# Chunk-selected attention and a hard-swish MLP in one kernel: longer K rows, a different split of the batch 0 bounds, a third transposed group by DMA, another last tile, and a new order

## The chip, the cores and the metric

The kernel runs on one core of a Trainium2 chip. The time is the device time of one execution in microseconds. One execution was also taken by the hardware profiler; its times are us from the start of the profiled span. The engines are PE (TensorE: matmuls and transposes; PEld is its weight load), DVE (VectorE), ACT (ScalarE), POOL (GpSimd) and SP (SyncE, which here issues nearly all DMAs; a few early ones come from ACT).

## The reference

Four batches, 8 heads, 768 positions, head size 64. K is cut into 24 chunks of 32 positions. For each query an upper bound of its scores with each chunk is worked out from the chunk's minimum and maximum, the 6 best chunks at or before its own are kept, and attention runs on those alone, causally. The result, as 3,072 rows of 512, goes through a two-layer MLP.

```python
k_min, k_max = np.min(k_chunks, axis=3), np.max(k_chunks, axis=3)
ub = np.sum(np.maximum(q * k_min, q * k_max), axis=-1)      # per query and chunk
ub = np.where(causal, ub, -1e9)
top_chunks = np.argsort(ub, axis=-1)[..., -6:]
scores = np.where(sel & causal_positions, scale * q @ k.T, -1e9)
x = softmax(scores) @ v            # as 3072 x 512
h = x @ w_in                       # 512 x 2048
g = h * np.clip(h + 3, 0, 6) / 6
out = g @ w_out                    # 2048 x 512
```

Queries 0 to 191 have at most six chunks, so bounds are needed for the 576 others.

## The kernel before, in words

**An order written out.** All work is a list of tokens (`ORDER`), each of which calls one small function; the functions' instructions are appended to their engines' queues in the list's order, and each engine runs its own queue in that order, waiting where an operand is not there or a buffer is not free. A token's last letter is a PSUM place: a, b, c are tiles of two banks, x and y single banks. There is no planner at build time: the list is the schedule, for the queues of SP and POOL too.

**Batch 0 (four head pairs, tokens in capitals).** `AQ`, `LK`, `LQ`, `LV` load half of a head's q, k or v (96 KB, rows of 256 bytes, L379 and L388). `KT`, `QT` transpose them on PE (L398) with an identity that POOL makes (`PI`); `MX`, `MN` reduce K's chunks to maximum and minimum on DVE (L412); `KB`, `QB` cast to bf16 on ACT. `UH.i.h` computes the bounds of pair i (L440): the low half (h=0) has 192 queries, two column groups of 96; the high half (h=1) has 384, two column groups of 192. `UB` adds the causal bias (L446; bias made by POOL, `PB`, L266 to L271), `TH` transposes (L454), `T8` takes the top eight (L461), `SE` compares (L465), `LH` and `MT` bring the mask back (L471, L475). The chunk indicator `EM`, which turns a mask into additions to the scores, is cut by POOL (`PC`, L278, L280) and copied to four partition groups (`EG`, L288).

**Batches 1 to 3 (six quads of four heads, n = 2 to 7, tokens in small letters).** `lk.n`, `lq.n` load K or Q of a quad, four DMAs of 192 KB, 32 positions to a partition group per head, rows of 256 bytes (L222), into one of three slabs of the staging buffer, which batch 0's halves also use. `kd`, `qd` turn 32 x 32 blocks on DVE (L228); `kb`, `qb` cast on ACT (L303); `mx`, `mn` reduce (L311), `kx` takes the span (L316), `rp` the positive part of Q (L322). `ud.n` computes the bounds (L333, 128 small matmuls), `us`, `tr`, `tm`, `se`, `tb` bias, turn, select and turn back on DVE, `mv` moves mask rows on POOL (L363), and `SQ.n.u` computes the scores of four heads for one of six units (L510, L514).

**Attention and MLP.** `ex` is the exponential (ACT, L520), `af` the causal cut on POOL (L527), `A`, `B` the products with V for the low and high three query blocks (L543), `na`, `nb` the normalisation (DVE, L560, L563) into x. A group g of 384 rows (two to a batch) is transposed either on PE (`X.g.n`, two steps of six transposes, L576, copied by DVE, `xe`, L580: groups 0 to 2) or by three DMA transposes on SP (`xt.g`, L569: groups 3 to 7). `wl`, `wc` load a 1 MB weight chunk (L238) and cast it on POOL (L242): chunks 0 to 3 are w_in, of which `H.g.f` needs chunk f // 2; 4 to 7 are w_out, of which `O.g.t.n` needs chunk 4 + n. `H.g.f` is a hidden step (L587, 8 matmuls), `hu` (ACT, L595) and `gt` (DVE, L598) the gate, `O.g.t.n` a quarter of an output tile's projection (L625, 4 matmuls; n needs the gates 2n and 2n + 1), `ot` its unload on ACT (L632), `st` its store on SP (L636). One tile, `LAST`, is computed as two halves of 256 columns, each unloaded and stored by itself (L613 to L616). `LAST` is the tile of the list's last `st` token, which is (7, 0); but its steps stand ahead of those of tile (7, 2).

Of the kernel before, what the change touches and what calls it, by code (L numbers as in the profile page):

```python
# [9 lines left out]
A = mybir.AluOpType  # L10
# [5 lines left out]
P = 128  # L16
CH = 32
# [17 lines left out]
PW AQ.2.0.1 LK.0.0.0 PT PI PO LK.0.1.1 AQ.0.0.1 PR Z.y.6 PZ PF PB LK.0.0.1 KT.0.0.b PC AQ.0.0.0 MX.0.0 EG.2 LK.1.0.1  # L35
MN.0.0 EG.0 LK.1.0.0 PA EG.1 QT.0.0.y AQ.1.0.1 EG.3 AQ.1.0.0 LK.0.1.0 AQ.2.0.0 RP.0.0 RN.0.0 KT.1.0.a MN.1.0 MX.1.0
KB.0.0 QB.0.0 QT.1.0.x KT.0.1.y RP.1.0 KB.1.0 RN.1.0 UH.0.0.c UH.1.0.b QB.1.0 MN.0.1 KB.0.1 LQ.0.1.1 UB.1.0 UB.0.0
MX.0.1 LQ.0.1.0 QT.0.1.a RA.0.1 QB.0.1 RP.0.1 TH.1.0.b T8.1.0 TH.0.0.c LQ.3.0.1 T8.0.0 QT.2.0.x RP.2.0 SE.1.0
LQ.3.0.0 QT.3.0.y RP.3.0 LK.3.0.0 RN.2.0 SE.0.0 LK.2.0.1 UH.0.1.a LK.2.0.0 KT.2.0.b RN.3.0 LK.3.0.1 UB.0.1 QB.2.0
MN.2.0 QB.3.0 KT.3.0.c LQ.2.1.0 KB.3.0 LH.1.0.a MX.2.0 MT.1.0 KB.2.0 LQ.2.1.1 QT.2.1.y UH.2.0.a RP.2.1 RA.2.1 QB.2.1  # L40
MX.3.0 LK.3.1.0 LH.0.0.b MN.3.0 TH.0.1.x LQ.1.1.1 MT.0.0 S.0.1.b ex.0.1 UB.2.0 T8.0.1 SE.0.1 S.0.0.a ex.0.0 LK.1.1.0
af.0.0 LQ.1.1.0 QT.1.1.c RN.1.1 QB.1.1 TH.2.0.y RP.1.1 LH.0.1.b LK.1.1.1 KT.1.1.x T8.2.0 SE.2.0 UH.3.0.a LH.2.0.y
MT.0.1 LV.3.0.1 KB.1.1 LV.0.0.0 LK.2.1.1 S.1.1.b UB.3.0 ex.1.1 af.1.1 MT.2.0 MN.1.1 S.0.5.c LK.2.1.0 MX.1.1 KT.2.1.y
MN.2.1 MX.2.1 S.1.0.a TH.3.0.x ex.0.5 ex.1.0 UH.1.1.b T8.3.0 S.2.1.c SE.3.0 UB.1.1 UH.2.1.a UB.2.1 af.0.5 LH.3.0.b
MT.3.0 TH.1.1.x af.0.1 ex.2.1 KB.2.1 af.2.1 T8.1.1 S.2.0.c TH.2.1.y af.1.0 ex.2.0 lk.2 LV.3.0.0 S.0.3.b ex.0.3
S.0.4.c SE.1.1 T8.2.1 SE.2.1 LH.1.1.x MT.1.1 LK.3.1.1 ex.0.4 LV.0.0.1 VC.0.0 KT.3.1.a MN.3.1 A.0.y LV.1.0.1 na.0
KB.3.1 S.3.1.b ex.3.1 S.3.0.c LQ.3.1.0 LV.1.0.0 LQ.3.1.1 QT.3.1.x MX.3.1 RN.3.1 ex.3.0 VC.1.0 af.2.0 A.1.y na.1
RP.3.1 LH.2.1.b MT.2.1 S.1.3.a ex.1.3 S.1.4.c LV.2.0.0 kd.2.1 X.0.0.y xe.0.0 ex.1.4 UH.3.1.b UB.3.1 af.3.1 mx.2.1
S.1.5.a S.1.2.c QB.3.1 VC.3.0 af.3.0 A.3.y na.3 LV.2.0.1 ex.1.5 af.1.3 ex.1.2 VC.2.0 A.2.x S.0.2.b ex.0.2 TH.3.1.y
na.2 S.2.3.c ex.2.3 T8.3.1 LV.0.1.1 SE.3.1 wl.0 S.2.5.a X.0.1.x xe.0.1 S.2.2.b ex.2.2 LH.3.1.y MT.3.1 wc.0 af.0.2  # L50
wl.1 kd.2.0 mx.2.0 H.0.1.c hu.0.1 ex.2.5 gt.0.1 mn.2.0 af.1.2 af.0.3 LV.0.1.0 VC.0.1 B.0.0.x H.0.0.b hu.0.0 gt.0.0
wc.1 B.0.1.x nb.0 H.0.2.c hu.0.2 mn.2.1 gt.0.2 S.3.3.b ex.3.3 S.3.2.a ex.3.2 LV.1.1.1 LV.1.1.0 VC.1.1 kb.2.1 af.1.5
kb.2.0 wl.2 wc.2 B.1.0.y B.1.1.y nb.1 lk.3 S.3.5.b af.3.2 kd.3.1 mn.3.1 bd ex.3.5 af.3.5 H.0.4.c hu.0.4 gt.0.4
mx.3.1 H.0.3.a S.2.4.b af.2.2 ex.2.4 kd.3.0 kx.2 mx.3.0 wl.3 H.0.5.c hu.0.5 gt.0.5 hu.0.3 af.2.5 lq.2 gt.0.3 wc.3
H.0.6.b hu.0.6 S.3.4.c qd.2.1 af.3.3 ex.3.4 LV.3.1.0 H.0.7.a gt.0.6 af.2.3 rp.2.1 qd.2.0 LV.3.1.1 VC.3.1 LV.2.1.1
X.1.0.c xe.1.0 B.3.0.x LV.2.1.0 B.3.1.x kb.3.0 VC.2.1 B.2.0.y B.2.1.y nb.3 rp.2.0 ud.2.c.b nb.2 hu.0.7 wl.4 gt.0.7
X.1.1.x xe.1.1 H.1.3.a hu.1.3 us.2.1 qb.2.0 us.2.0 tr.2.1 H.1.1.b hu.1.1 tm.2.1 wc.4 mn.3.0 O.0.0.0.y se.2.1 gt.1.3
gt.1.1 tb.2.1 mv.2.3 lq.3 qd.3.0 qd.3.1 wl.5 H.1.6.c kb.3.1 hu.1.6 gt.1.6 O.0.2.0.x tr.2.0 kx.3 H.1.5.a hu.1.5
# [53 lines left out]
def kernel(  # L112
# [580 lines left out]
```

## Time and profile before

| what | us |
|---|---|
| median of 3 runs (275.39 to 277.91) | 275.52 |
| the profiled execution | 275.69 |
| its span | 274.0 |
| PE busy in the span | 261.3 |
| DVE busy | 184.0 |
| ACT busy | 181.0 |
| POOL busy | 102.6 |
| share of the 16 DMA engines taken by SP's queue | 56.6% |
| bytes read from HBM, written | 27.26 MB, 6.29 MB |

The granted TensorE clock is 1.00 throughout. A profile line of groups has the line, engine, operation, output and inputs with shapes, the count, then the busy time and the mean ns of one, then the idle time of the engine just before them and what ended it. In the list of busy time by stretch, each engine has its busy us and (x instructions), and the last three columns are the granted clock, the share of the DMA engines' time and GB/s. The chain of work that ended last is followed back from the end, from each piece of work to what released it. PE is "busy" from a matmul's start to its modelled end.

### The profile page before, as it was taken

Reading aid. Unit: us, or ns where it says so; the run is one execution under the profiler, and the core shown is the slowest. Engines: PE = TensorE matmul, PEld = TensorE weight load, DVE = VectorE, ACT = ScalarE, POOL = GpSimd, SP = SyncE. Lnnn points to the kernel's source line nnn. Section 1 sums busy time; section 2 is a strip of 40 time slices with the busy share of each in tenths; the row PEclk is TensorE's granted clock in tenths of the full one; section 3 lists DMA queues with packets and bytes.
Section 4 is the critical chain, followed back from the end, with each engine's and each line's share of the span. In section 5 each row is a group of like instructions: output and inputs, shape, how many; then the busy total and the mean of one; then the engine's idle time right before and its main releaser. Section 6 shows DMA issues by size and latency. Waiting matters only on the chain.

```text
span 274.0 us, 8574 instructions
## 1 busy us (share of the span) xinstructions
PE 261.3 (95%) x3550; PEld 153.7 (56%) x3550; DVE 184.0 (67%) x452; ACT 181.0 (66%) x249; POOL 102.6 (37%) x241
## 2 busy tenths in 40 slices
PE   6998997899999999999999999998999999999994
PEld 3666765565545565664545655464655565555561
DVE  4898998999899779867874788575662423342620
ACT  2798978647499894878578746992887634325610
POOL 7215686325777552532825232421544310000000
PEclk9999999999999999999999999999999999999999
DMA  8999999998996999139900449114212044003002
GB/s 164 205 180 163 335 250 252 219 286 246 261 184 190 160 212 186 36 76 171 231 4 28 107 103 173 40 21 99 79 52 47 2 133 100 0 2 115 38 22 97
DMA packets 91479, 36.08 MB, mean 132 GB/s; under 512 B 84144, under 2 KB 84400, under 8 KB 91440
## 3 DMA queue, kind: packets, MB, share of 16 engines
q1 hardware_dynamic: 89040, 34.94, 56.6%
q10 hardware_dynamic: 2400, 0.59, 1.2%
q8 instruction: 28, 0.46, 0.8%
q14 instruction: 11, 0.09, 0.1%
HBM read 27.26 MB, written 6.29 MB: 122 GB/s over the span
## 4 chain that ended last, share of the span: by engine, by line
PE 76%; DMA 13%; SPq 3%; DVE 3%; POOL 1%; ACT 1%; issue 1%; DVEq 0%
PE PSy L625 15%; PE PSx L625 10%; PE PBa L587 10%; PE PBc L587 9%; PE PBb L587 8%; DMA WS<-in_moe_w_in_dram 4%; DMA STAGE<-in_q_dram 4%; DMA STAGE<-in_k_dram 3%; PE PBa L510 3%; PE PSx L543 2%; PE PSy L543 2%; PE PBc L625 2%; PE PBc L510 2%; PE PBb L510 2%; PE PBb L333 2%; DMA XT<-XB 1%
## 5 line engine op out<-in xcount | busy, mean ns | idle before, releaser
L587 PEld LDWEIGHTS <-WIN 128*128 128x128 bf16 x512 | 48.9, 98 | 37.7 <-issue 4.2
L527 POOL TENSOR_SCALAR_AFFINE_SELECT PT<-PT 128x256 bf16<-128x256 bf16 x78 | 30.2, 409 | 70.2 <-ACT PT L520 69.9
L625 PEld LDWEIGHTS <-GT 128*128 128x128 bf16 x368 | 33.1, 98 | 37.8 <-issue 2.4
L625 PE MATMUL PSy<-WOUT,GT 128*128 128x512 bf16 x192 | 46.8, 380 | 0.0
L363 POOL COPY MQ<-MTM 32x144 bf16<-32x144 bf16 x96 | 29.1, 304 | 31.3 <-DVE MTM L357 27.5
L587 PE MATMUL PBc<-XT,WIN 128*128 128x384 bf16 x184 | 33.7, 326 | 1.4 <-DVE GT L598 1.4
L598 DVE SCALAR_TENSOR_TENSOR GT<-U,PBa 128x768 bf16<-128x768 bf16 x22 | 20.9, 948 | 19.8 <-ACT U L595 19.8
L587 PE MATMUL PBa<-XT,WIN 128*128 128x384 bf16 x176 | 32.4, 326 | 1.3 <-DMA XT<-XB 0.7
L625 PE MATMUL PSx<-WOUT,GT 128*128 128x512 bf16 x128 | 31.8, 380 | 0.0
L598 DVE SCALAR_TENSOR_TENSOR GT<-U,PBc 128x768 bf16<-128x768 bf16 x23 | 21.8, 947 | 10.4 <-ACT U L595 10.3
L520 ACT ACTIVATE PT<-PBb 128x1024 bf16<-128x1024 f32 (+2 forms) x26 | 23.6, 908 | 7.6 <-PE PBb L514 5.3
L587 PE MATMUL PBb<-XT,WIN 128*128 128x384 bf16 x152 | 27.8, 326 | 0.2 <-POOL WIN L242 0.2
L595 ACT ACTIVATE U<-PBc 128x768 bf16<-128x768 f32 x23 | 18.7, 812 | 13.9 <-PE PBc L587 10.2
L598 DVE SCALAR_TENSOR_TENSOR GT<-U,PBb 128x768 bf16<-128x768 bf16 x19 | 18.1, 951 | 13.6 <-ACT U L595 13.6
L595 ACT ACTIVATE U<-PBa 128x768 bf16<-128x768 f32 x22 | 17.9, 812 | 13.5 <-PE PBa L587 13.5
L520 ACT ACTIVATE PT<-PBc 128x1024 bf16<-128x1024 f32 (+2 forms) x26 | 24.2, 930 | 3.5 <-PE PBc L497 1.3
L520 ACT ACTIVATE PT<-PBa 128x1024 bf16<-128x1024 f32 (+2 forms) x26 | 23.9, 921 | 3.8 <-PE PBc L514 2.0
L228 DVE STREAM_TRANSPOSE STAGE<-STAGE 128x768 f32<-128x768 f32 x24 | 22.7, 960 | 1.7 <-DMA STAGE<-in_k_dram 1.3
L595 ACT ACTIVATE U<-PBb 128x768 bf16<-128x768 f32 x19 | 15.4, 812 | 12.1 <-PE PBb L587 12.1
L311 DVE TENSOR_REDUCE KMA<-STAGE 128x24 f32<-128x768 f32 x24 | 22.3, 941 | 0.1
L543 PEld LDWEIGHTS <-PT 128*128 128x128 bf16 x546 | 19.0, 97 | 3.6 <-issue 0.7
L510 PEld LDWEIGHTS <-KBA 32*128 32x128 bf16 x480 | 9.4, 92 | 14.7 <-issue 11.7
(192 smaller groups left out, 460.3 us busy)
## 6 DMA issues: line engine op xcount, KB each, us to landing
out_dram<-OT SPq DMA_DIRECT2D x23, 256.0 KB, 2.5
STAGE<-in_k_dram SPq DMA_DIRECT2D x24, 192.0 KB, 5.0
STAGE<-in_q_dram SPq DMA_DIRECT2D x24, 192.0 KB, 5.5
VS<-in_v_dram SPq DMA_DIRECT2D x12, 384.0 KB, 4.2
WS<-in_moe_w_in_dram SPq DMA_DIRECT2D x4, 1024.0 KB, 7.0
WS<-in_moe_w_out_dram SPq DMA_DIRECT2D x4, 1024.0 KB, 6.7
STAGE<-in_k_dram SPq DMA_DIRECT2D x16, 96.0 KB, 3.2
VS<-in_v_dram SPq DMA_DIRECT2D x16, 96.0 KB, 4.2
```

What stands on the lines that cost most here:

```text
L228: nc.vector.transpose(out=T, in_=T)
L311: nc.vector.tensor_reduce(out=dst, in_=staged("k", n)[:, h], axis=AX.X, op=(A.max, A.min)[w])
L333: nc.tensor.matmul(PSB[(c, cc)[g // 2]][CH * part:CH * (part + 1), g % 2, 0:NQ // 4], lhsT=KM4[n % 2][rows, w, x, :], rhs=R[rows, :, x, 8 ...
L363: nc.gpsimd.tensor_copy(MQ[n % 2][CH * g:CH * (g + 1), w * part:w * (part + 1)], MT4[n % 2][CH * part:CH * (part + 1), w * g:w * (g + 1)])
L510: nc.tensor.matmul(PSB[both[g // 2]][:, g % 2, at:at + w], lhsT=K[rows, x, j * P:(j + 1) * P], rhs=Q[rows, x, q0:q0 + w], start=(x == 0), ...
L520: nc.scalar.activation(pt(i, u)[:, :, 0:n], PSB[slot["S", i, u]][:, :, 0:n], ACT.Exp, scale=float(scale))
L527: nc.gpsimd.affine_select(out=T[:, :, lo:lo + P], in_=T[:, :, lo:lo + P], pattern=[[0, 2], [1, P]], compare_op=A.is_ge, fill=0.0, base=0, ...
L543: nc.tensor.matmul(O[:, e, t, :], lhsT=pt(i, u)[:, e, lo:lo + P], rhs=VB[i % 4][:, j, e, :], start=(j == 0), stop=(j == qb))
L587: nc.tensor.matmul(PSB[c][:, ff, 0:GRP], lhsT=WIN[:, kt, (2 * f + ff) * P:(2 * f + ff + 1) * P], rhs=XT[g % 3][:, kt, :], start=(kt == 0), ...
L595: nc.scalar.activation(slot["R", g, f][:], PSB[slot["H", g, f]][:, :, 0:GRP], ACT.Relu, bias=3.0)
L598: nc.vector.scalar_tensor_tensor(out=GT[g % 2][:, 2 * f:2 * f + 2, :], in0=slot["R", g, f][:], scalar=6.0, in1=PSB[slot["H", g, f]][:, :, ...
L625: nc.tensor.matmul(PSS[c], lhsT=GT[g % 2][:, f, t * P:(t + 1) * P], rhs=WOUT[:, f, :], start=(f == 0), stop=(f == FT - 1))
```

## The change

Token for token the work is the same, but for `X.2.0`, `X.2.1`, `xe.2.0` and `xe.2.1`, which go, and `xt.2`, which comes. The other edits:

- **K of quads 2 and 3** is loaded so that each row of a DMA is four positions, 1,024 bytes, over all 128 partitions: six DMAs of 128 KB instead of four of 192 KB. The positions then lie in another sequence in the slab, so the cast becomes two instructions per half (which put them back in sequence), and the reduce two per half, each over four pieces of eight elements. The turn on DVE stays.
- **High bounds of batch 0** go in four column groups of 96 queries instead of two of 192: 16 matmuls instead of 8, the bias add on 128 x 192 instead of 64 x 384, two transposes instead of four. The bias on POOL takes six selects instead of four.
- **Group 2 of x** goes by DMA transposes.
- **The split tile** is (7, 2), the last one computed, with its halves in the two banks of one PSUM tile.
- Buffers of the quads' bounds are joined (the turn is done in place), and mask rows go in a ring of three.
- **The order** is new from the first token to the last.

```diff
+    LONG = (2, 3)
+    R4 = 4
+    def slab(m, n):
+        at = (1 + 2 * (n - FIRST_QUAD) + "kq".index(m)) % 3
+        return FLAT[:, 2 * S * at:2 * S * (at + 1)]
+    def long_rows(n):
+        return slab("k", n).rearrange("p (u r x t) -> p x u r t", r=R4, x=2, t=CH)
...
+            if m == "k" and n in LONG:
+                src = x[b, first:first + 4].rearrange("g (u t r) d -> u g t (r d)", t=CH, r=R4)
+                dst = slab("k", n).rearrange("p (u y) -> p u y", y=R4 * D)
+                for u in range(S // (CH * R4)):
+                    nc.sync.dma_start(dst[:, u], src[u])
+                return
...
+            if m == "k" and n in LONG:
+                dst = KB4[n % 2].rearrange("p x (u t r) -> p x u t r", t=CH, r=R4)[:, :, 3 * h:3 * h + 3]
+                src = long_rows(n)[:, :, 3 * h:3 * h + 3]
+                for x in range(2):
+                    (nc.scalar.copy if engine == "act" else nc.gpsimd.tensor_copy)(
+                        dst[:, x], src[:, x].rearrange("p u r t -> p u t r"))
+                return
...
+            if n in LONG:
+                for x in range(2):
+                    src = long_rows(n)[:, x, 3 * h:3 * h + 3].rearrange("p u r (c t) -> p u c r t", c=R4)
+                    nc.vector.tensor_reduce(out=dst[:, x].rearrange("p (u c) -> p u c", c=R4), in_=src, axis=AX.XY, op=op)
+                return
...
-            for g in range(2):
-                lo = Q0 * h + n * g
+            for g in range(2 * (h + 1)):
+                lo = first_query(h, g) - Q0
...
-        for h, cc in enumerate((c, "abcxy"["abcxy".index(c) + 1])):
+        for h in range(2):
+            bank = PSB[c][:, h, :]
...
-    LAST = [tuple(int(x) for x in t.split(".")[1:3]) for t in ORDER if t.startswith("st.")][-1]
+    LAST = (2 * B - 1, TPG - 1)
```

Stretches of the new order that the prediction speaks of: the start, the way to the first quad's bounds, group 2 of x, and the end.

```
AQ.2.0.1 PB LK.1.0.1 PT PF LK.0.0.0 AQ.0.0.0 LK.1.0.0 LK.0.1.1 PA LK.0.0.1 PZ AQ.1.0.1 PW Z.c.6 AQ.0.0.1 PO PC EG.2
AQ.1.0.0 LK.0.1.0 AQ.2.0.0 EG.3 PI PR KT.1.0.a MN.1.0 MX.1.0 KT.0.0.x MN.0.0 KB.1.0 QT.0.0.y RP.0.0 MX.0.0 KB.0.0
...
hu.0.6 lq.2 qd.2.1 rp.2.1 qd.2.0 rp.2.0 gt.0.6 H.0.7.a hu.0.7 nb.3 nb.2 wl.4 ud.2.c.b mx.3.0 bd us.2.0 wc.4 X.1.1.y
xe.1.1 gt.0.7 wl.5 O.0.2.0.x O.0.0.0.y H.1.6.c hu.1.6 wc.5 us.2.1 tr.2.0 tm.2.0 se.2.0 tb.2.0 mv.2.0 mv.2.1 qb.2.1
...
af.6.0 A.6.y mx.5.1 SQ.3.4.b.a ex.6.4 af.7.0 A.7.c ex.7.4 na.6 O.1.1.3.x ot.1.1 O.1.2.0.y na.7 SQ.3.3.c.b ex.6.3
af.5.3 af.5.5 B.5.0.x O.1.2.1.y kd.5.0 SQ.3.5.a.c ex.7.3 af.7.3 O.1.2.2.y O.1.2.3.y ex.6.5 lq.5 qd.5.1 tm.4.1 se.4.1
xt.2 ex.7.5 lv.8 af.7.5 ot.1.2 H.2.2.b H.2.3.c tb.4.1 B.4.0.y B.4.1.y lv.9 af.6.5 mv.4.0 mv.4.1 rp.5.1 hu.2.2
...
gt.7.7 H.7.0.b st.6.1 hu.7.0 H.7.4.a gt.7.0 hu.7.4 gt.7.4 st.6.2 H.7.6.c O.7.0.0.x O.7.0.1.x O.7.1.0.y O.7.0.2.x
O.7.1.1.y O.7.1.2.y st.6.0 hu.7.6 gt.7.6 O.7.0.3.x ot.7.0 st.7.0 O.7.1.3.y ot.7.1 st.7.1 O.7.2.0.c O.7.2.1.c
O.7.2.2.c O.7.2.3.c ot.7.2 st.7.2
```

In the order before, the loads on SP ran `lk.2` ahead of the last three loads of batch 0's K and Q and all but two halves of V, then, behind most of V, `wl.0`, `wl.1`, `wl.2`, `lk.3`, `wl.3`, `lq.2`, the last four halves of V, `wl.4`, `lq.3`, `wl.5`. In the new one `wl.0` stands ahead of all but one half of V, then come `lk.2` and `lk.3` among the halves of V, `wl.1`, the last two halves, `wl.2`, `wl.3`, `lq.2`, `wl.4`, `wl.5`, `lq.3`.

223 lines of the change are left out of this document (107 added, 116 removed).

## The prediction

> **What bounds the kernel now.** The profile's page first: in 40 slices, PE is busy nearly throughout, DVE and the DMA engines only in the first third.
>
> ```profile
> PE   6998997899999999999999999998999999999994
> DVE  4898998999899779867874788575662423342620
> DMA  8999999998996999139900449114212044003002
> ```
>
> Next the busy time by stretch (each engine's busy us and count, then clock, DMA share, GB/s).
>
> ```profile
> 17.40:52.40 35.00, 31.33 (x485) 21.61 (x486) 32.13 (x87) 28.72 (x39) 21.05 (x38) 1.00 1.03 238
> 55.80:270.20 214.40, 212.91 (x2858) 120.39 (x2858) 135.88 (x307) 138.92 (x185) 73.40 (x184) 1.00 0.49 109
> ```
>
> From 55.8 to 270.2 PE idles 1.5 of 214.4 us: there only PE's own work, or a wait removed there, shortens anything. Before that PE is not the limit: from 17.4 to 52.4 the DMA share is 1.03 and DVE is busy 32.13 of 35. The chain of work that ended last agrees. It ends the head with a DMA and a short way to the first bounds of quad 2 (`ud.2`, L333):
>
> ```profile
> 44.62 7.67 DMA STAGE<-in_q_dram
> ...
> 52.42 0.98 DVE STAGE L228
> 53.39 0.47 DVE GT L598
> ...
> 54.16 0.97 DVE STAGE L228
> ...
> 55.73 0.31 PE PBc L333 x2
> ```
>
> The Q rows of quad 2 land at 52.29, DVE turns both halves (L228) and gates one hidden tile between (L598), and `ud.2` starts at 55.73. So the run is a head, ended by `ud.2`, then 214.4 us of dense PE, then 3.8 us of tail. The profiled execution took 275.69 us, its span 274.0, so 1.7 lie around the span; the median of the runs is 275.52, 0.17 less. I sum against 275.69.
>
> **The long K rows.** What the loads deliver depends on their rows; windows again, then the stores of the two 128 KB halves, whose rows have 1,024 bytes:
>
> ```profile
> 1.30:17.90 16.60, 14.23 (x145) 9.16 (x146) 12.73 (x54) 10.60 (x24) 6.55 (x13) 1.00 0.99 190
> 29.40:32.40 3.00, 3.00 (x64) 2.07 (x63) 2.92 (x6) 3.00 (x5) 0.86 (x2) 1.00 1.04 398
> ```
>
> ```profile
> GB/s 0 0 0 0 0 0 0 0 0 0 0 0 0 0 0 0 137 300 396 300 369 151 69 14 14 0 0 0 0 0 0 0 0 0 0 0 0 0 0 82
> ```
>
> 256-byte rows (1.3 to 17.9) give 190 GB/s at a DMA share of 0.99; the 2,048-byte rows of w_in give 398. Rows of 1,024 bytes lie between; the slices of the half tile's store (265 to 268 us) reach 300 to 396, so I take 350. A half load (98,304 bytes) is then 0.52 us, K or Q of a quad (786,432 bytes) 4.14, a chunk of w_in 2.63, K of a quad in long rows 2.25 (1.98 to 4.14).
>
> Ahead of Q of quad 2 and with it, the queues carried 44 half loads (32 of K and Q, 12 of V), two K and one Q of a quad, and four chunks: 22.9 + 12.4 + 10.5 = 45.8. Measured, from 1.3 to 52.29, it is 51.0, or 1.11 times that. The new order puts all 16 V halves ahead: 48 half loads, two long K, one Q, four chunks: 25.0 + 4.5 + 4.1 + 10.5 = 44.1, times 1.11 is 49.1, so Q lands at 50.4 (49.8 at 398 GB/s, 54.7 at 190). The saving on K is 4.2, and the four V halves take half of it back. SP issues 12 K loads instead of 8, but the DMA share of 1.03 says that loads stand queued all this time.
>
> **DVE is the other bound of the head.**
>
> ```profile
> 1.08 0.29 POOL masks.py:199 TENSOR_SCALAR_AFFINE_SELECT IDENT<-IDENT 128x128 f32<-128x128 f32 x1
> ...
> 1.72 1.35 POOL L271 TENSOR_SCALAR_AFFINE_SELECT BIASM<-BIASM 32x96 f32<-32x96 f32 x4
> ...
> 3.63 0.85 POOL L278 TENSOR_SCALAR_AFFINE_SELECT XT<-XT 32x768 bf16<-32x768 bf16 x1 [0.57 <-DVE XT L275]
> ...
> 5.47 3.43 POOL L288 COPY EM<-XT 32x768 bf16<-32x768 bf16 x4
> 5.47 0.87 PE L398 MATMUL PBb<-IDENT,STAGE 128*128 128x128 f32 x3 [1.47 <-POOL XT L280]
> ...
> 6.38 1.02 DVE L412 TENSOR_REDUCE KMA<-PBb 128x12 f32<-128x384 f32 x2 [2.82 <-PE PBb L398]
> ```
>
> The identity was ready at 1.4. Now POOL first does the bias (a memset and six selects instead of four, some 2.2 us from 0.8), two selects (1.8) and two of the four EM copies (1.7): the identity comes at about 7.0, the first transposes at 7.1 instead of 5.47, and the first DVE reduce 1.6 later than 6.38.
>
> ```profile
> L311 DVE TENSOR_REDUCE KMA<-STAGE 128x24 f32<-128x768 f32 x24 | 22.3, 941 | 0.1
> L303 ACT CAST KBA<-STAGE 128x768 bf16<-128x768 f32 x12 | 9.9, 832 | 0.0
> L412 DVE TENSOR_REDUCE KMA<-PBa 128x12 f32<-128x384 f32 x4 | 2.1, 550 | 0.0
> L446 DVE TENSOR_TENSOR UBM<-PBa,BIASM 64x384 f32<-64x384 f32 x2 | 1.1, 547 | 0.3 <-PE PBa L440 0.3
> L446 DVE TENSOR_TENSOR UBM<-PBa,BIASM 64x192 f32<-64x192 f32 x2 | 0.7, 342 | 0.0
> ```
>
> A long quad's reduce becomes two of 384 elements per half. No row has their pieces of eight; the lower end is the 0.94 of one L311, the upper two whole ones, 1.88. I take the pair of L412 just shown, 1.02, as it is the nearest in size: +0.08 each for the six ahead of Q of quad 2 (+0.5). Four column groups halve the free size of the four high bias adds: 0.547 to 0.342 each, -0.8. Ahead of that Q also moves one more reduce (`mn.3.0`) and one X copy, and two reduces (`mx.3.0`, `mx.3.1`) move behind: about -0.5. Together -0.8. DVE had 2.87 us idle in 17.4 to 52.4, so by work alone it could have turned Q at 49.6; now 49.6 + 1.6 - 0.8 = 50.4, the moment Q lands. They meet; for the waits that remain I add 0.8 (0 to 2.4) and take 51.2. Then two turns and a gating, 0.9 each, in one row (that last gating frees bank c, which `ud.2` writes first): `ud.2` at 53.9 instead of 55.73, **-1.8** (from -2.8 to +1.7). The ACT casts of the long K, two instead of one, cost between nothing and 0.83 more for each of the four, 3.3 at most, inside ACT's 6.3 idle us of the 35: nothing, and at worst late by what DVE already is. The bounds in four column groups and the two larger transposes save PE time in the head, where PE waits anyway: nothing. The weights' first chunk now goes ahead of most V; its three followers land later than before and `H.0.3`, `H.0.4`, `H.0.6` come just behind their casts, still ahead of 51.2.
>
> **The dense part.** The PE steps behind `ud.2` are the same ones but for `X.2.0` and `X.2.1`, six transposes each:
>
> ```profile
> 98.89 0.34 PE PBc L576 x6
> ...
> 100.69 0.44 PE PBb L576 x6
> ```
>
> That is **-0.8**, and 1.1 us of DVE copies, hidden. Three DMA transposes on SP replace them (median us to landing, then the time of the issue):
>
> ```profile
> XT<-XB SPq DMA_TRANSPOSE x15, 2.5
> ```
>
> ```profile
> L569 SPq DMA_TRANSPOSE XT<-XB x15: 1196/1260/1885, 120.8 to 228.6; - x15
> ```
>
> ```profile
> 182.40 0.57 DVE XB L563
> ...
> 183.02 1.20 SPq L569
> ...
> 189.79 1.46 PE PBa L587 x8
> ```
>
> ```profile
> PE PBa L587 <- DMA XT<-XB: 0.7, 1, 0.7
> ...
> PE PBa L587 <- DVE XT L580: 0.3, 1, 0.3
> ```
>
> Once, in group 5, x was ready at 182.97 and the hidden matmuls began at 189.79, 6.8 later and 0.7 late. In the new order `na.7` ends some 0.8 behind `A.7`; from `A.7` to `H.2.2` PE has five projection steps (0.87 each, a quarter of the 3.47 below), two quad scores and one values step, 6.3 in all as the same steps take in this trace. x lands between 5.2 (two issues of 1.2 and 1.26, a landing of 2.5, hand-overs) and 6.8 behind `na.7`, so 6.0 to 7.6 behind `A.7`: 0 to 1.3 late, I take **+0.4**. On SP, `lq.5` is ahead of it, whose buffer `kb.4.0` freed before; behind it wait `lv.8`, `lv.9`, `st.1.2`, not due for many steps. [...]
>
> In the new order group 5's high values end several steps ahead of `H.5.4`, so that **0.7** wait goes; so does the **0.3** on the X copy, which `O.0.2.0` and `O.0.0.0` now cover. The other tight place is `ud.3`: Q of quad 3 lands two chunks and one Q later, 9.4 x 1.11 behind 50.4, at 60.8; then DVE owes seven operations of 0.9 or so and a short one, to 67.4, while PE gets there at 68.3 (bounds 1.9, six hidden steps of 1.31, five projections, one step of transposes: 14.4 behind 53.9). I allow **+0.25** for such places.
>
> **The tail.**
>
> ```profile
> 257.67 1.31 PE PBb L587 x8
> ...
> 261.73 1.47 PE PBc L625 x6
> ...
> 266.69 3.47 PE PBb L625 x16
> 270.18 0.60 ACT OT L632
> ```
>
> ```profile
> 264.98 0.39 ACT L615 ACTIVATE OT<-PSx 128x256 f32<-128x256 f32 x1 [1.15 <-PE PSx L613]
> ```
>
> ```profile
> out_dram<-OT SPq DMA_DIRECT2D x23, 256.0 KB, 2.5
> ...
> out_dram<-OT SPq DMA_DIRECT2D x2, 128.0 KB, 1.8
> ```
>
> Behind the last hidden step (end 258.98) the 16 matmuls of tile 7.1 should take 3.47 but end at 263.20: 0.75 lost to gating. Now six projection steps stand between the last hidden step and the step that needs its gate, 5.2 us against some 1.8 of ACT and DVE: **-0.75**. The split tile is now the last: its unload takes 0.39 instead of 0.60, and the last store lands in 1.8 instead of 2.5: **-0.9**.
>
> **Sum:** -1.8 - 0.8 - 0.7 - 0.3 - 0.75 - 0.9 + 0.4 + 0.25 = -4.6; 275.69 - 4.6 = 271.1. Its own range is 269.0 to 272.7.
>
> **Rivals.** *Long rows save nothing.* At 190 GB/s Q lands at 54.7 and `ud.2` starts at 57.4, 3.5 later than forecast: 274.6. For it speaks that the same bytes go into the same buffer in more and smaller loads; against it the store's 300 to 396. [...]
>
> *The x group comes late.* SP takes its queue in order; if an earlier load or store holds it 3 us past `na.7`, `H.2.2` waits 3.4 instead of 0.4: 274.1. For it speaks the 0.7 of group 5, against it that its predecessors' buffers are free by then.
>
> *Slower: the reduces over pieces of eight.* Place: DVE, six pairs ahead of `ud.2`, two ahead of `ud.3`. Every 0.1 us of a pair beyond 1.02 moves the end by up to 0.8. From about 1.6 us a pair the change costs time; at 1.88, the upper end, it gives 271.1 + 8 x 0.86 = 278.0, and at 2.0 it is 278.9. For it speaks that no row shows this view; against it that a reduce of 384 out of PSUM and one of 768 out of SBUF go at 1.4 and 1.2 ns an element.
>
> **How the numbers follow.** My forecast 0.62; better than its range 0.04 (all of the unknown costs at their low end); long rows without effect 0.14; late x group 0.12; reduces 0.08. About 1%, 2.8 us, is what a measurement of this kernel can tell from no change: faster is below 272.8, slower above 278.3. Faster takes the first two and half of the late x group, 0.72; slower most of the reduces, 0.07; 0.21 remain. The range, 268.8 to 274.9, leaves out the reduces, the best end and a little of the others.
>
> **What would show it.** Right: K loads of quads 2 and 3 above 300 GB/s, Q of quad 2 landed by 51, `ud.2` near 54, LONG reduces near 0.55 us each, no wait over 0.3 on the gate in the last 15 us, under 3 us from the last matmul to the end. Wrong: first bounds later than 55.7; a wait on `DMA XT<-XB` over 1 us in group 2; PE idling over 3 us between 54 and 265.

## The result, and the profile after

The changed kernel takes 285.55 us (median of four executions, 283.99 to 286.61), the kernel before 275.62 beside it: a ratio of 1.0336, 95% interval 1.0263 to 1.0409. It is slower; 271.1 was predicted. Executions of one kernel scatter by 1 to 2% here; the ratios below leave disturbed ones out, so a ratio can stand a little off the medians beside it.

The profiled execution took 286.61 us, 10.9 more than that of before. The first bounds of quad 2 (`ud.2`) start at 65.76 instead of 55.73: +10.0. From there to the end of the last matmul it takes 215.9 instead of 214.4: +1.5. From there to the end of the span it takes 3.2 instead of 3.8: -0.6. So the loss lies ahead of `ud.2`. The page's slices of the span first:

```profile
PE   3899954988999999898999999999999999999994
DVE  3779862999999978476699944781294232524620
PEclk9999995999999999999999999999999999999999
DMA  8994338989988985836960349520400031400303
```

The DMA digits fall to 4, 3, 3 where before had 9s, from 21 to 43 us (a slice is 7.1 us); from 36 to 50 PE has a 5 and a 4, and in the second of these slices its clock has a 5. Busy time by stretch, for the kernel before and then the changed one (the last three columns are granted clock, DMA share, GB/s; in this stretch the kernel before also moves weights, in rows of 2,048 bytes):

```profile
24.00:40.00 16.00, 15.17 (x252) 10.97 (x250) 15.40 (x43) 13.62 (x18) 10.65 (x19) 1.00 0.89 265
```

```profile
24.00:40.00 16.00, 15.11 (x358) 11.25 (x357) 14.72 (x60) 15.82 (x23) 8.18 (x18) 1.00 0.35 104
...
39.40:46.40 7.00, 0.34 (x11) 0.26 (x6) 0.75 (x3) 3.79 (x5) 0.62 (x2) 0.74 0.59 143
46.40:52.00 5.60, 5.51 (x73) 4.09 (x73) 3.65 (x8) 0.81 (x1) 4.70 (x9) 0.72 1.07 385
```

While the long K rows are under way (24 to 40 us) the DMA engines are busy for a third of their time and move 104 GB/s instead of 265. From 39.4 to 46.4 PE does next to nothing, and when it goes on, its clock is 0.72 on average (0.50 up to 49.6, then 1.00). What it waits for, in PE's list of waits (who waited, on whom; us in all, times, longest) and then in POOL's order of time:

```profile
PE PSy L575 <- POOL VB L425: 6.7, 1, 6.7
PE PBc L305 <- DVE XT L259: 3.1, 1, 3.1
PE PBa L431 <- POOL IDENT masks.py:199: 1.4, 1, 1.4
PE PBc L359 <- DVE RINV L592: 1.2, 1, 1.2
PE PSx L658 <- DVE UBM L368: 0.9, 1, 0.9
PE PBb L619 <- ACT OT L665: 0.8, 1, 0.8
```

```profile
36.45 1.49 POOL L559 TENSOR_SCALAR_AFFINE_SELECT PT<-PT 128x256 bf16<-128x256 bf16 x4
45.78 0.51 POOL L425 CAST VB<-VS 128x384 bf16<-128x384 f32 x1 [7.84 <-DMA VS<-in_v_dram]
```

PE waits 6.7 us for a cast of V, and POOL had waited 7.84 for the V half to land. That half stands on SP's queue behind the six loads of K of quad 3. Last, the two groups of instructions that work on the long K: ACT's casts and DVE's reduces.

```profile
L318 ACT CAST KBA<-STAGE 128x384 bf16<-128x384 f32 x8 | 6.5, 872 | 0.0
L335 DVE TENSOR_REDUCE KMA<-STAGE 128x12 f32<-128x384 f32 x16 | 7.9, 542 | 0.0
```

A half costs ACT 1.74 instead of 0.83, DVE 1.08 instead of 0.94. Two pairs of these casts lie on the chain that leads from the late V cast to `ud.2`:

```profile
53.91 1.55 ACT KBA L318 x2
...
56.75 1.07 ACT KBA L318 x2
...
65.76 0.31 PE PBc L359 x2
```

**Theory 1**: each long load covers four heads, so the slowest dimension of its source is 4, and it runs on four of the sixteen DMA engines. The trace's records of single DMA rows point that way: a row of 1,024 bytes takes an engine 46 ns (median), in these loads as in the half tile's stores of the kernel before, but of the 19 us in which such loads are under way, exactly four or five rows are in flight in 15.5 and never more than six. Four engines at 46 ns would give 4 x 1,024 / 46 = 89 GB/s, an estimate that takes each row in flight for one engine, since the records don't name the engine; the 104 above include other loads. **Theory 2**: the identity comes late and TensorE starts slow (three transposes take 0.85 to 0.90 us up to 18.7 us, 0.49 at 19.7). **Theory 3**: the new order puts K ahead of V, and V would be late with any rows. **Theory 4**: the casts and reduces for the new layout are the loss.

### The profile page after: what moved, and what is told of

It reads as the page before. It is cut to its first block, busy times and chain, and to the rows that moved or that the text cites. A ratio compares the mean times of both kernels' runs of the same rounds, so it can differ in the third digit from the quotient of the medians.

```text
span 284.9 us, 8698 instructions
## 1 busy us (share of the span) xinstructions
PE 263.8 (93%) x3594; PEld 155.1 (54%) x3594; DVE 182.5 (64%) x458; ACT 183.2 (64%) x253; POOL 102.8 (36%) x243
## 4 chain that ended last, share of the span: by engine, by line
PE 79%; DVE 7%; ACT 5%; issue 5%; POOL 2%; ACTq 0%; DVEq 0%; POOLq 0%
PE PSy L658 13%; PE PSx L658 10%; PE PBc L619 9%; PE PBa L619 9%; PE PBb L619 8%; PE PSx L575 3%; PE PBb L658 3%; PE PBc L542 2%; PE PBb L542 2%; PE PBa L542 2%; ACT PT L552 2%; PE PSy L575 2%; DVE GT L630 1%; PE PBc L359 1%; PE PBc L646 1%
## 5 line engine op out<-in xcount | busy, mean ns | idle before, releaser
L619 PEld LDWEIGHTS <-WIN 128*128 128x128 bf16 x512 | 49.1, 98 | 36.3 <-issue 2.4
L658 PEld LDWEIGHTS <-GT 128*128 128x128 bf16 x368 | 33.1, 98 | 38.8 <-issue 3.8
L658 PE MATMUL PSy<-WOUT,GT 128*128 128x512 bf16 x176 | 43.7, 380 | 0.0
L658 PE MATMUL PSx<-WOUT,GT 128*128 128x512 bf16 x144 | 35.4, 380 | 0.9 <-DVE UBM L368 0.9
L619 PE MATMUL PBc<-XT,WIN 128*128 128x384 bf16 x184 | 33.7, 326 | 0.5 <-DVE KMA L342 0.5
L619 PE MATMUL PBa<-XT,WIN 128*128 128x384 bf16 x176 | 32.2, 326 | 0.3 <-DVE GT L630 0.3
L630 DVE SCALAR_TENSOR_TENSOR GT<-U,PBa 128x768 bf16<-128x768 bf16 x22 | 20.9, 949 | 14.5 <-ACT U L627 14.5
L630 DVE SCALAR_TENSOR_TENSOR GT<-U,PBb 128x768 bf16<-128x768 bf16 x19 | 18.0, 949 | 17.3 <-ACT U L627 17.2
L619 PE MATMUL PBb<-XT,WIN 128*128 128x384 bf16 x152 | 27.8, 326 | 0.8 <-ACT OT L665 0.8
L552 ACT ACTIVATE PT<-PBb 128x1024 bf16<-128x1024 f32 (+2 forms) x23 | 21.8, 949 | 10.1 <-PE PBb L529 7.7
L627 ACT ACTIVATE U<-PBc 128x768 bf16<-128x768 f32 x23 | 18.7, 813 | 13.3 <-PE PBc L619 13.3
L552 ACT ACTIVATE PT<-PBa 128x1024 bf16<-128x1024 f32 (+2 forms) x28 | 25.8, 921 | 1.9 <-PE PBb L546 1.4
L630 DVE SCALAR_TENSOR_TENSOR GT<-U,PBc 128x768 bf16<-128x768 bf16 x23 | 21.7, 944 | 6.3 <-ACT U L627 6.2
L575 PEld LDWEIGHTS <-PT 128*128 128x128 bf16 x546 | 19.8, 99 | 10.9 <-issue 7.5
L239 DVE STREAM_TRANSPOSE STAGE<-STAGE 128x768 f32<-128x768 f32 x24 | 22.7, 960 | 1.4 <-DMA STAGE<-in_q_dram 1.1
L542 PE MATMUL PBb<-QBA,KBA 32*128 32x384 bf16 (+2 forms) x168 | 16.3, 276 | 0.0
```

The lines of the kernel that those rows point to most:

```text
L239: nc.vector.transpose(out=T, in_=T)
L542: nc.tensor.matmul(PSB[both[g // 2]][:, g % 2, at:at + w], lhsT=K[rows, x, j * P:(j + 1) * P], rhs=Q[rows, x, q0:q0 + w], start=(x == 0), ...
L552: nc.scalar.activation(pt(i, u)[:, :, 0:n], PSB[slot["S", i, u]][:, :, 0:n], ACT.Exp, scale=float(scale))
L575: nc.tensor.matmul(O[:, e, t, :], lhsT=pt(i, u)[:, e, lo:lo + P], rhs=VB[i % 4][:, j, e, :], start=(j == 0), stop=(j == qb))
L619: nc.tensor.matmul(PSB[c][:, ff, 0:GRP], lhsT=WIN[:, kt, (2 * f + ff) * P:(2 * f + ff + 1) * P], rhs=XT[g % 3][:, kt, :], start=(kt == 0), ...
L627: nc.scalar.activation(slot["R", g, f][:], PSB[slot["H", g, f]][:, :, 0:GRP], ACT.Relu, bias=3.0)
```

## The experiments

**heads.** The long rows stay, but each load covers one head:

```diff
-                src = x[b, first:first + 4].rearrange("g (u t r) d -> u g t (r d)", t=CH, r=R4)
                 dst = slab("k", n).rearrange("p (u y) -> p u y", y=R4 * D)
-                for u in range(S // (CH * R4)):
-                    nc.sync.dma_start(dst[:, u], src[u])
+                for g in range(4):
+                    nc.sync.dma_start(dst[CH * g:CH * (g + 1)],
+                                      x[b, first + g].rearrange("(u t r) d -> t u (r d)", t=CH, r=R4))
```

> The changed kernel, with K of quads 2 and 3 still in 1,024-byte rows, but loaded head by head: four transfers of 196,608 bytes that begin with 32 rows each, instead of six whose slowest dimension is the four heads. Theory 1 (a transfer whose slowest dimension is 4 is spread over only four of the sixteen DMA engines, so that the long loads go at about 100 GB/s and hold the V halves behind them): the DMA share while they are under way goes from 0.2 to 0.35 back to 0.9 or more, the 6.7 us for which TensorE waits for a V cast at 39.6 fall to under 1.5, the first bounds of quad 2 come at 55 to 58 instead of about 65.8, time 275 to 278. Theory 2 (the late identity and the cold TensorE of the first 19 us are the main loss): no change, 285. Theory 3 (the new order itself, with K of quad 2 ahead of most V halves, makes V late): the wait shrinks by less than half, 282 to 285.

Measured: 276.09, ratio 1.0000 (0.9958 to 1.0042). Its stretch from 24 to 40:

```profile
24.00:40.00 16.00, 15.47 (x378) 11.73 (x379) 14.70 (x60) 15.81 (x22) 8.91 (x24) 1.00 0.77 185
40.00:52.00 12.00, 11.38 (x141) 7.70 (x138) 11.78 (x21) 10.97 (x15) 7.37 (x10) 1.00 0.99 294
```

The wait for V is gone (PE is busy 11.38 of the next 12 us, at full clock), up to 21 rows of 1,024 bytes are in flight at once, and `ud.2` starts at 57.5. The same bytes in rows of the same length, with the same casts and reduces in the same order, and some 9.5 us less: the four heads in front of each load, theory 1, are the main cause, and the three others are not. The DMA share is 0.77, not the 0.9 expected; that comes up again below. The profiled execution was one of the longer ones, 278.94.

**short.** The same order with 256-byte rows (`LONG = ()`).

> The changed kernel with K of all quads in 256-byte rows, as in the kernel before (16 engines, some 190 GB/s, one ACT cast and two reduces of 768 elements per half instead of pairs); the order and everything else as changed. Theory 1 (four engines): K of a quad takes 4.1 us instead of some 7 to 8, the DMA share is near 1 throughout, the V cast that TensorE waits for comes 5 to 7 us sooner, time 276 to 279, so most of the loss goes with the long rows alone. Theory 3 (the order): V is still behind K, the wait stays over 4 us, 282 to 285. Theory 4 (strided casts and reduces of long K load ACT and DVE): the casts fall from 1.6 to 0.83 a half; if that were the loss, 280 or less with the wait on V unchanged.

Measured: 280.04, ratio 1.0135 (1.0075 to 1.0195); `ud.2` at 60.4. So most of the loss goes with the long loads; this edit takes their casts and reduces away too, but heads, which keeps them, is no slower than the kernel before. Theory 3 has a part: with K ahead of V and of the weights (and with the change's other edits, which are in this run too), short rows cost 1.35%. In this order long rows, loaded well, are worth 4 us.

**b_long.** The kernel before, with nothing but the change's long loads, casts and reduces.

> The kernel before with one part of the change alone: K of quads 2 and 3 in 1,024-byte rows as the change loads them, with the casts and reduces for that layout; its own order, bounds, masks and tail. Theory 1 (four engines): each K of a quad takes 3 to 4 us longer and Q of quad 2 stands behind two of them, so the first bounds of quad 2 go from 55.7 to 61 to 64, time 281 to 285. Theory 3 (the new order): here V halves are ahead of the K loads, so the time is as before or better, 273 to 276.

Measured: 285.33, ratio 1.0328 (1.0291 to 1.0365), `ud.2` at 66.1: the whole loss from this one part, in the old order too, which speaks against theory 3 as the main cause. The part contains the casts and reduces; the run b_heads, below, has them with the other loads and stands at 1.0115.

**ident.** The changed kernel with the identity and the warm-up first:

```diff
-AQ.2.0.1 PB LK.1.0.1 PT PF ... PW Z.c.6 AQ.0.0.1 PO PC EG.2 ... EG.3 PI PR KT.1.0.a
+PW AQ.2.0.1 LK.1.0.1 PT PI ... PR ... Z.c.6 PF PB ... PO PC EG.2 ... EG.3 KT.1.0.a
```

> The changed kernel with the identity made first on GpSimd, as in the kernel before, the bias and chunk masks behind it, and the warm-up's zeros first on VectorE; loads and all else as changed. Theory 2 (late identity, cold TensorE): the first transposes come 1.5 us sooner, at about 5.5, matmuls run at full clock from about 12 instead of 17 to 19, and the time falls by 2 to 4, to 282 to 283. Theory 1 (four engines): what TensorE gains in the first 20 us it waits longer for the V cast at 39 to 46, whose data the DMA queue sets; under 1 us gained, 284.5 to 286.

Measured: 286.91, ratio 1.0361 (1.0323 to 1.0398). The first transposes came at 5.41 instead of 7.20, and `ud.2` at 66.4 as before. The earlier start on PE brought nothing while the loads were late: theory 2 is not the cause.

**heads_ident.** Both edits.

> The run of the long loads by heads, and the identity first on GpSimd with the warm-up's zeros first on VectorE. Theory 2, now that the DMA no longer hides it: in the run by heads TensorE's first transposes began at 7.18 instead of 5.47 and ran at half speed to 16, VectorE began 1.7 later, and VectorE is busy without a gap up to the first bounds of quad 2; so the first bounds come 1.5 to 2.5 sooner than 57.5, at 55 to 56, and the time is 273 to 274.5. Rival (the Q rows of quad 2, which land at 54.65 in the run by heads, set the first bounds by themselves, whatever VectorE does): the gain ends at about 57, under 0.7 us, 275.4 to 276.1.

Measured: 277.78, ratio 0.9993 (0.9952 to 1.0035); `ud.2` at 58.2. The rival's account fits: Q of quad 2 landed at 55.29, and the first bounds came 2.9 later. PE gained little from its earlier start, too: the transposes took 0.85 to 0.91 up to 17.5 us, and 0.49 from 18.4.

**warm.** In addition ten warm-up matmuls (`Z.c.10`), and the last tile's halves in two PSUM tiles (next run).

> The changed kernel with the long loads by heads, the identity first, the last tile's halves in two PSUM tiles, and ten warm-up matmuls instead of six. Theory (the clock of TensorE in the head: six warm-up matmuls of 0.46 us end at 4.0 and leave a gap before the first transposes, after which TensorE needs until 9, 10, 15 or 18 us, by chance, to reach full speed): ten of them end at about 5.6 and are long enough by themselves, the transposes run in 0.55 instead of 0.9 from the first, TensorE reaches its steps at 20 us some 2.3 us sooner than with six, the first bounds of quad 2 come at 55.5 to 56.5, the executions scatter less, and the time is 272 to 274. Rival (what is gained at 20 us is lost again where VectorE and the weights set the pace, before the first bounds): first bounds at 57.5 or later, 275 to 277.

Measured: 277.25, ratio 1.0005 (0.9970 to 1.0040); the profiled execution took 274.91, with `ud.2` at 56.1. PE's first rows, and those of the changed kernel:

```profile
1.26 4.45 PE L305 MATMUL PBc<-XT 128*128 128x512 bf16 x10 [1.26 <-DVE TINY L262]
5.50 0.64 PE L431 MATMUL PBa<-IDENT,STAGE 128*128 128x128 f32 x3
6.58 0.52 PE L431 MATMUL PSx<-IDENT,STAGE 128*128 128x128 f32 x3 [0.44 <-DMA STAGE<-in_k_dram]
```

```profile
7.20 0.90 PE L431 MATMUL PBa<-IDENT,STAGE 128*128 128x128 f32 x3 [1.41 <-POOL IDENT masks.py:199]
...
17.84 0.90 PE L431 MATMUL PBb<-IDENT,STAGE 128*128 128x128 f32 x3
19.72 0.49 PE L431 MATMUL PSx<-IDENT,STAGE 128*128 128x128 f32 x3
```

The transposes go as expected (0.49 to 0.55 from 6.6 us on, where the changed kernel still has 0.90 at 17.84 and 0.49 only at 19.72), the gain in time isn't there: over twelve executions no difference. The trace doesn't settle where it goes. Its `ud.2` is where the theory put it, but the profiled execution is the shortest of the twelve, and in cast and k_plain, which start in the same way, `ud.2` came at 57.1 and 58.0, nearer to the rival's 57.5.

**b_warm.** The kernel before with `Z.y.10` alone.

> The kernel before with ten warm-up matmuls instead of six and nothing else. There TensorE is at full speed from 9.2 us in the profiled execution. Theory (a longer warm-up is worth what TensorE gains up to 20 us, and VectorE and the loads set the head of the kernel before): within 1 us of the kernel before, 274.5 to 277. Rival (the warm-up alone is worth the 2 us that are expected of it in the changed kernel): 273 to 274.

Measured: 276.99, ratio 1.0012 (0.9980 to 1.0043). No difference, as the theory had it.

**tail.** heads_ident with the halves of the last tile in two PSUM tiles:

```diff
-            bank = PSB[c][:, h, :]
+            bank = (PSB[c][:, 0, :], PSS["x"])[h]
```

> The run by heads with the early identity, and the two halves of the last tile summed in two PSUM tiles (c and x) instead of the two halves of one, so that the second half need not wait until ScalarE has read the first. Theory (the wait in front of the second block of sixteen matmuls, 0.5 us, comes from the shared tile): the last matmul ends 0.4 to 0.8 us sooner than with the same head and the shared tile. Rival (the wait is for the weights or the gate): no difference.

Measured: 278.15, ratio 0.9945 (0.9886 to 1.0003), too wide for a verdict on the time. The two blocks of the last tile show it, first in the changed kernel, then here:

```profile
277.37 1.91 PE L646 MATMUL PBc<-WOUT,GT 128*128 128x256 bf16 x16
279.75 1.91 PE L646 MATMUL PBc<-WOUT,GT 128*128 128x256 bf16 x16 [0.47 <-ACT OT L648]
```

```profile
271.55 1.91 PE L646 MATMUL PBc<-WOUT,GT 128*128 128x256 bf16 x16
273.30 1.91 PE L646 MATMUL PSx<-WOUT,GT 128*128 128x256 bf16 x16
```

From one block to the next it is 2.38 with a shared tile and 1.75 with two: 0.6 us, a wait that the change added and the prediction had not seen.

**q_early.** heads_ident with Q of quad 2 ahead of the fourth weight chunk:

```diff
-mx.2.1 wc.2 wl.3 wc.3 ... hu.0.6 lq.2 qd.2.1
+mx.2.1 wc.2 lq.2 wl.3 wc.3 ... hu.0.6 qd.2.1
```

> The run by heads with the early identity, and the four loads of Q of quad 2 ahead of the fourth chunk of w_in on SyncE's queue instead of behind it. Theory (SyncE stands up to 5.2 us at the fourth chunk, whose staging buffer waits for a cast on GpSimd, with Q behind it, so a freed DMA engine has nothing to move): Q lands by 50 instead of 54.65, the first bounds of quad 2 come 0.5 to 1.5 us sooner than with the same head alone, and the time falls by as much. Rival (VectorE's work sets the first bounds): Q lands as early, the first bounds and the time stay within 0.5 us.

Measured: 281.62, ratio 1.0194 (1.0156 to 1.0232). Q landed at 51.07 instead of the 55.29 of heads_ident, and `ud.2` came at 62.0: neither account. The fourth chunk now stood behind Q, and the third shared the DMA engines with it: POOL cast them at 48.66 and 54.81 instead of 46.81 and 51.22, and the hidden steps ahead of `ud.2` waited for these casts:

```profile
PE PBc L619 <- POOL WIN L253: 3.4, 1, 3.4
PE PBb L619 <- POOL WIN L253: 1.8, 1, 1.8
```

**b_heads.** The kernel before with the long rows loaded by heads.

> The kernel before with one part of the change alone, mended: K of quads 2 and 3 in 1,024-byte rows loaded head by head (16 engines), with the casts and reduces for that layout; its own order otherwise. By the prediction's sum for this part alone the two K loads save 4.2 us of DMA time ahead of Q of quad 2, of which VectorE's work lets some 2 through: 273 to 274.5. Rival (what limits the loads is that SyncE stands at waits for staging buffers, so bytes saved only make the queue idle): no change, 275 to 276.5. Second rival (the strided casts, 1.6 us a half instead of 0.83, hold ACT): 276 to 278.

Measured: 278.66, ratio 1.0115 (1.0054 to 1.0176). Q of quad 2 landed at 50.36 instead of 52.29, and yet `ud.2` came at 56.8 instead of 55.7: the second rival's side. The four executions lie in two pairs, 277.0 and 277.3, then 280.0 and 280.7, so the ratio is less sure than its interval says.

**b_plain.** The same loads with the casts and reduces of the old layout. This leaves out what puts the positions back in sequence, so K of these quads is not the reference's: the run shows times alone.

> The kernel before with K of quads 2 and 3 in 1,024-byte rows loaded head by head, as in the run b_heads, but with the casts and reduces of the old layout (one cast of 768 elements and one reduce of 768 a half), so that the keys of those quads come out in another order: this leaves the computation wrong and shows the loads alone. Theory A (the loads save time and the casts in pairs, 0.88 each instead of one of 0.83, take it back): the first bounds come at 53.5 to 55 instead of 56.84, time 273 to 275.5. Theory B (K's loads were not what the first bounds waited for): first bounds at 55.5 to 57, time 275.5 to 277.5, no better than before.

Measured: 276.05, ratio 0.9982 (0.9950 to 1.0013), Q at 50.31, `ud.2` at 56.2. Against b_heads, the casts and reduces of the new layout are what probably made it slower; against the kernel before, Q lands 2.0 sooner and nothing comes of it. DVE's order of time ahead of `ud.2`:

```profile
48.35 1.68 DVE L344 TENSOR_TENSOR KMA<-KMA 128x48 f32<-128x48 f32 x1
49.95 0.94 DVE L339 TENSOR_REDUCE KMA<-STAGE 128x24 f32<-128x768 f32 x1
50.81 0.94 DVE L626 SCALAR_TENSOR_TENSOR GT<-U,PBc 128x768 bf16<-128x768 bf16 x1
51.67 0.94 DVE L626 SCALAR_TENSOR_TENSOR GT<-U,PBa 128x768 bf16<-128x768 bf16 x1
52.54 0.96 DVE L243 STREAM_TRANSPOSE STAGE<-STAGE 128x768 f32<-128x768 f32 x1
```

No row has a wait: DVE comes to Q's first turn (L243) at 52.54, two us after Q landed. In the old order DVE's work sets `ud.2` as soon as the loads don't: theory B. A part of that work is a coincidence with POOL: the first row took 1.68, where the kernel before has 0.37 (what ran beside it, the last section has). Without these 1.3 us DVE would have come to Q at 51.2, still 0.9 behind its landing, and `ud.2` at 54.9, 0.8 ahead of the kernel before (estimates from these figures). So it is the time, more than this one trace, that speaks for theory B.

**k_plain.** The run warm with the casts and reduces of the old layout; it leaves out the same as b_plain.

> The run with ten warm-up matmuls and the long loads by heads, with the casts and reduces of the old layout, so that the keys of quads 2 and 3 come out in another order (computation wrong, as in the run before this one). Theory A: ScalarE has 3.4 us less to do ahead of the first bounds, VectorE 0.6 less, the first bounds come 1 us or more sooner than 56.12 and the time is 1 to 2 us under that run. Theory B (V, weights and VectorE's other work set the head): within 0.5 us of that run.

Measured: 275.91, ratio 0.9971 (0.9937 to 1.0005) against 1.0005 for warm: no difference that can be told. Here `ud.2` came at 58.0 and Q landed at 55.05. In the new order, with Q where the change has it, the first bounds follow Q's landing by 2.9 us in most of these runs: 54.56 and 57.50 in heads, 57.45 and 60.40 in short, 53.18 and 56.12 in warm, 55.05 and 58.00 here. So there the loads set them, and the casts are hidden. Only in cast (next) is it 3.8, 53.26 and 57.1. Q's own landing differs by 2 us between runs that load it in the same way.

**cast.** The run warm with the casts walking 32 neighbouring elements at a time.

> The kernel of the run with ten warm-up matmuls, with ScalarE's casts of the long K walking in the other order: 32 neighbouring elements of the source at a time, the result scattered by four, instead of every 64th element of the source and a result without gaps. Theory (the step between neighbours on the source side is what makes a cast of 384 elements take 0.87 us, where one of 768 takes 0.83): a cast falls to 0.45 to 0.5 us, the eight casts save 3 us of ScalarE, and the time falls by 0 to 1 us against that run. Rival (the price is one of the shape, three dimensions, on either side): 0.8 to 0.9 us as before, no difference.

Measured: a cast takes 1.10 instead of 0.88, so the theory is wrong, and the rival's 0.8 to 0.9 is as well; the time, 277.20 with a ratio of 0.9958 (0.9918 to 0.9997), does not differ from that of warm.

**b_tail** and **b_tail2.** The kernel before with the last tile split (`LAST = (2 * B - 1, TPG - 1)`), each half in its own tile; in b_tail2 the store of tile 7.0 also goes ahead of it.

> The kernel before with one part of the change alone: the last tile summed and stored in halves, each half in its own PSUM tile, instead of the tile two before it. Theory (the prediction's term for the tail without its new order): from the last matmul's end to the end of the span 3.86 us become 3.0 to 3.3, and the time falls by 0.5 to 0.9. Rival (what is left out at the end comes back in front of it, since the second block of sixteen matmuls of 256 columns takes 0.1 us more than the whole tile's): under 0.3.

> The run b_tail with the store of tile 7.0 issued ahead of the last tile's halves, so that the last thing on SyncE's queue is a store of half a tile. Theory (the prediction's tail: unload of half a tile 0.39 instead of 0.60, landing of half a tile in 1.8 instead of 2.5): from the last matmul's end to the end of the span 3.86 us become 3.0 to 3.3; the time falls by 0.5 to 0.9 against the kernel before, at the edge of what the rounds can tell. Rival (the end after the last landing costs as much as before, whatever lands last): 3.6 to 3.9, no difference.

Measured: 276.47, ratio 0.9996 (0.9968 to 1.0024), and 275.71, ratio 0.9971 (0.9939 to 1.0003). From the last matmul's end to the end of the span, 4.1 and 3.3 us, against 3.84. In b_tail SP issued the whole tile's store last, at 271.12, behind the halves: the split bought nothing. In b_tail2 it is 0.5 shorter.

No version is clearly faster than the kernel before: tail, cast and b_tail2 (and k_plain, which computes something else) come out 0.3 to 0.55% lower, and of their intervals only that of cast, one of many, ends below 1, at 0.9997.

## Why the prediction was wrong

**What bounds the kernel** was read rightly: a head that ends with `ud.2`, then dense PE. 10.0 of the 10.9 us lost lie ahead of `ud.2`.

**The step that failed: "so I take 350" for the long rows.** 53.9 was predicted for `ud.2`, 65.76 measured. The time of a row was right: the stores that served as its model and the long loads have the same 46 ns. But the stores begin with 128 rows and spread (up to 19 rows in flight at once), the long loads begin with 4 (four or five). The sum treated the rate as a matter of the row's length alone; how many rows are in flight at once was a factor of four beside it, and the 190 at the low end of the range could not hold 104. heads and b_long show it from both sides.

**"Loads stand queued all this time" failed too**, in the new order. With the loads mended, the profiled execution of heads (278.94) is 7.8 over the 271.1: `ud.2` comes 3.6 late, and the dense part takes 4.2 more than predicted. Q of quad 2 landed at 54.56, not 50.4. The stretch up to Q's landing, in the kernel before, in heads and in warm:

```profile
1.30:52.29 50.99, 44.95 (x620) 30.37 (x621) 44.37 (x138) 38.74 (x61) 27.55 (x50) 1.00 1.02 223
```

```profile
1.30:54.56 53.26, 46.78 (x741) 32.47 (x742) 45.27 (x145) 40.74 (x65) 28.54 (x54) 1.00 0.90 223
```

```profile
1.30:53.18 51.88, 46.53 (x746) 31.42 (x747) 43.59 (x144) 41.47 (x65) 28.56 (x54) 1.00 0.99 235
```

In heads the DMA engines had nothing to move for some 5 us of 53. A part is from 27 to 31 us (share 0.60), behind a stand of SP for a V buffer:

```profile
SPq L421 <- POOL VB L425: 2.3, 2, 2.0
```

But a queue that is never empty isn't enough: in warm the share is 0.99, and Q still landed at 53.18. The queues of SP and ACT had moved 12.1 MB by then, where the loads that the prediction counts (48 halves, two K, one Q, four chunks) are 11.3. The other 0.8 MB belong to loads that stand behind Q on SP's queue: they share the engines with it. At the 398 GB/s of the prediction's line they are 2 us, an estimate. The kernel before shows the same, 11.3 MB for the 10.9 counted, so the sum charged the last four halves of V, 0.4 MB, to the new order alone.

**ACT's casts "between nothing and 0.83 more": nothing taken.** The 0.91 more measured is above that range. In the changed kernel, behind the late V, two pairs lie on the chain to `ud.2`. With the loads mended they probably cost in the old order (b_heads against b_plain), and in the new one nothing shows (k_plain against warm).

**The reduces** at 1.08 a pair for 1.02 predicted were right, and the rival built on them was dead. **The late identity** was worked out rightly: the first transposes came at 7.20 (7.1 predicted), the first DVE reduce 1.8 later (1.6). That the transposes would then take 0.85 to 0.90 up to 18.7 us, and 0.49 only at 19.7, was not foreseen; ident, warm and b_warm show no gain in time without it.

**The dense part** was to be 1.9 shorter and is 1.5 longer. The transposes of group 2 went, and the gate's wait ahead of the last tile too: no wait at L658 over 0.3 behind 270 us. x of group 2 was late as foreseen, by 0.8 instead of 0.4: the third DMA transpose landed at 115.74 and the hidden step began at 115.88. The profile names `ACT OT` for it (L619, 0.8), which works on another bank; in cast the same step waits 0.8 as well and begins 0.14 behind the landing, in heads and warm it doesn't wait. PE idles 3.2 us in this part, for 1.5 before. New are the 0.5 at the shared tile (0.6 from block to block), 0.6 at the first bounds of quad 3, one of the tight places for which 0.25 was allowed, and 0.9 at a projection; which edit of the order made this last one was not tried. The part scatters from trace to trace: 213.8 to 215.5 in the runs with the old order and short K rows, 214.0 (warm) to 217.2 (tail) in the four with the new order and two tiles at the end. So the 1.9 shorter was not seen in any of them, and of the 1.5 longer a part is chance. In heads, 216.7, 1.0 goes at the first bounds of quad 3, and 1.2 inside those of quad 5, where the profile shows nothing that PE waited for.

**The tail** gave 0.6 of the 0.9. Its means were right (b_tail2), its size wasn't.

**The rivals.** None was right. "Long rows save nothing" comes nearest, but as a rate of 190, not as a loss.

## What to carry to other kernels

Before a load is reshaped, write down the first dimension of every transfer, not only the bytes of a row: here four heads in front went with four or five rows in flight, a DMA share of 0.35 and 104 GB/s from 24 to 40 us, and one loop over the heads made that 0.77 and 185. When bytes are saved on a queue, look at what the queue's issuer waits for and at what the next engine does when the data lands: here Q landed 2 us sooner in the old order (b_plain) and nothing came of it, because VectorE was not there yet. Count what stands behind a load on its queue as well: here 0.8 MB of it moved before the load had landed, an estimated 2 us. A change of order has a price of its own: read it with the suspected edit taken out.

## What the runs showed of the hardware

**In two runs the granted clock halved behind a wait of PE.** In the changed kernel PE stopped at 39.7, the granted clock fell to 0.50 at 42.8, 3.1 us after PE's last matmul, and was 1.00 again from 49.6, 3.2 us after PE went on at 46.3. In b_long PE waited 4.0 us, to 56.1, and the clock was 0.50 from 54.8, 2.6 us after the last matmul, to 61.6: a hidden step of eight matmuls took 2.72 there, 1.46 before the wait. What sets these times was not shown. With six warm-up matmuls three transposes took 0.85 to 0.91 up to 9.5 us in ident and up to 17.5 in heads_ident, which start in the same way, and 0.55 or less from 10.7 and 18.4; with ten they took 0.49 to 0.55 from 6.0 to 6.7 on (b_warm, warm, cast).

**Three times a small DVE instruction lasted as long as POOL's cast.** The chunk span, 128 x 48, takes 0.2 to 0.5 where no weight cast runs on POOL. In heads it began while one ran, and lasted 1.30, until that ended:

```profile
50.75 1.89 POOL L253 CAST WIN<-WS 128x2048 bf16<-128x2048 f32 x1 [2.20 <-DMA WS<-in_moe_w_in_dram]
```

```profile
51.40 1.30 DVE L342 TENSOR_TENSOR KMA<-KMA 128x48 f32<-128x48 f32 x1
```

In b_plain it lasted 1.68 (48.35 to 50.02) beside a cast from 48.08 to 49.96, in cast 1.43 (51.21 to 52.64) beside one from 50.69 to 52.58: each time it ended 0.06 behind the cast. Other DVE work beside such casts keeps its time in the traces of the kernel before and the changed one: a gating (L598, L630) takes 0.92 to 0.96 beside a cast and elsewhere, a turn (L228, L239) 0.94 to 0.97 beside one and 0.93 to 0.98 elsewhere, a reduce of 768 elements in the kernel before (L311) 0.94 to 0.96 and 0.91 to 0.96. Why the span is held up and these are not was not shown.
